# Causal masks of the last four attention units moved from TensorE to GpSimd, with a new instruction order, in an mLSTM plus two-MoE kernel

## The chip, the cores and the metric

One core of a Trainium2 chip runs the whole program. The metric is device time in microseconds (us) of one execution; lower is better. The engines are named as the profile names them: PE is TensorE (matmul), PEld its weight load, DVE is VectorE, ACT is ScalarE, POOL is GpSimd, SP is SyncE, from whose queue nearly all transfers (DMA) are issued.

## What is computed

An mLSTM layer (2 batches, 8 heads, 768 steps, head size 40), then two feed-forward layers on 1536 tokens of width 320. Cut to what matters:

```python
for t in range(S):                                   # attention part, per batch and head
    m_new = np.maximum(f_gate[:, :, t] + m, i_gate[:, :, t])
    f_stab = np.exp(f_gate[:, :, t] + m - m_new)
    i_stab = np.exp(i_gate[:, :, t] - m_new)
    C = f_stab * C + i_stab * outer(v_t, k_t)
    n = f_stab * n + i_stab * k_t
    y[:, :, t] = sigmoid(o_t) * (C @ q_t) / max(abs(n @ q_t), 1)
h = (x @ w1) * (x @ w2) @ w3                         # first MoE, x = y with heads joined
x = h @ w_out
h = x @ w_in                                         # second MoE
out = (h * tanh(softplus(h))) @ w_out2
```

All is float32. The kernel does not step through time: it cuts the 768 steps into 6 chunks of 128 and treats each chunk of a batch as masked attention plus a carried state.

## The kernel before

**Attention units.** There are 12 units, u = 0 to 11 (chunk u // 2 of batch u % 2), built by `add_unit`. The nodes of a unit, each a short list of instructions on one engine:

- `E` (PE): two products of 128x512 (`psE`, L469) that give the logarithms of the decay weights. Ahead of each stands a mask product (L468): the identity times a tile `causal`, which holds -1e30 where a key is later than a query. `dw` (ACT, L474) takes their exponential into the tile `w`.
- `S` (PE, L495): 8 products of keys and queries. `wg` (DVE, L499 to L501, shown as `w<-psS,w`) multiplies them into `w`, 2 instructions.
- `I` (PE, L506, L509): the carried state times the queries; `Ie` (DVE) scales it into `y`. `dx` (ACT) is a small exponential beside it.
- `vw` (POOL, L488) and `U` (PE, L520): the update of the state; `st` (DVE) applies it.
- `Y` (PE, L544): 8 products of `w` and the values; `cb` adds them to `y`.
- `r1`, `r2`, `r3` make 1/denominator; `xs` and `xo` (L572, L576, shown as `x<-y,sg` and `x<-x,r`) multiply `y` by the gate and by it; `dup` (ACT) copies a piece; `X` (PE, L588) transposes; `Xe` (ACT) and `Xl` (DVE) split the result in a high and a low part, which together carry float32 through products of a shorter type.

S, I, U and Y are plain float32: each of their matmuls stands twice in the trace, so a unit's 8 products are 16 rows.

**Weights.** `add_piece` loads a block of weights (SP), takes its bits apart (`mag` on ACT or DVE, then `clamp`, `bits1`, `bits2`, `bits` on DVE, L341 to L359, shown as `f`), and writes a high part (`hi`, ACT) and a low part (`lo`, DVE or POOL). There are 8 pieces each of w1 with w2 (`w12`) and of `w_in` (`wi`), 16 of w3 (`th`), 4 of `w_out` (`wo`) and 8 of `w_out2`.

**MoE stages.** `A` and `B` (PE, L903, `psa` and `psb`) are the products with w1 and w2: 8 matmuls of 128x512 each, for 8 blocks of columns and 3 groups of tokens, 24 of each. `Ae` (ACT) and `Be` (DVE) multiply them. `W` (PE, L876, `psw`) forms w3 @ w_out once, 16 runs of 12 matmuls; `X1` (PE, L943 to L948) applies it. `H` (PE, `psh`) and `O` (PE, L1018, `pso`) are the second MoE, 48 of each. The first A needs the attention output of units 0 to 3 only, so A and B of the first groups can stand between attention units.

**The order.** No engine chooses at run time: each runs its instructions in the order in which they were written down. A list scheduler inside the kernel (`Work.plan`, run while the kernel is built) makes that order from the nodes' due times (`TUNE`, plus `OFF`, an offset for single nodes), the engine of each node (`ENG`), and its own table of durations. Buffers (PSUM banks, `w`, `y`, `x`, weight slots) are given out in this order too. Where it sees TensorE idle before the last `X`, it writes in *warm products* (`keep_warm`, L440, `psz`): matmuls on constants whose result nobody reads. They hold up nothing but TensorE itself. `start` sets up constants, gates and their running sums on DVE and ACT.

The mask is chosen once for all units, by `ENG["mask"]` (L415); with any other value the node `ms` (L477 to L480) would set the masked part of `w` to zero on POOL by an affine select, for every unit.

Of the kernel before, what the change touches and what calls it, by code (L numbers as in the profile page):

```python
# [25 lines left out]
TUNE = dict(
    sgg=(2, 4), s_pe=0.0, s_act=0.143, s_dve=0.011, s_pool=0.0, ahead=3, w0n=8, ff=1.0, ph=3.235, a0=1273.88,
    ap=57.866, a_ld=-1806.87, e_e=2472.31, e_s=-765.62, e_r=7598.61, g_ld=-3051.46, g1=-3249.6, g2=-2767.38,
    o_1=-648.47, o_2=1399.95, c_ld=-2830.66, c_wo=6805.57, cp_wo=-37.478, p0=926.72, pp0=-60.314, c_12=-1429.3,
    w0=-11765.87, wp=-55.889, c_w3=286.38, p1=6793.31, pp1=56.325, p2=9829.98, pp2=563.967, x0=4913.06,  # L30
    x_p=-1108.66, x1=-8484.58, x2=-3892.43, xp=64.158, ldn=dict(w12=2, wi=2), c_o2=-6904.63, cp_o2=92.686,
    c_wi=6950.34, c_o3=10828.2, m0=-902.59, mp0=207.175, mp=248.708, m_o=2909.34,
)
# [10 lines left out]
OFF = dict(
    ll_1=3602.0, S_3=-1169.8, bits1_3=539.7, Y_0=2592.5, A_3=938.5, I_5=1807.9, lo_0=696.0, bits_1=575.3,
    Y_5=-246.0, X_5=621.3, r2_5=-605.0, X_6=-62.8, clamp_5=1680.0, S_7=-839.5, U_9=-210.4, B_0=574.8, lo_3=-503.5,
    xo_2=-1171.6, S_9=-129.5, Y_3=-649.9, mag_19=144.5, B_11=69.7, Y_7=74.1, lo_5=-87.0, clamp_7=73.7, r2_1=86.5,
    Xe_1=488.4, Y_2=-478.1, xo_1=-149.9, I_7=-61.8, st_4=404.5, I_4=-135.1, I_9=-47.3, A_13=-236.0, xs_7=31.9,
    X1h_0=-33.6, bits2_11=668.5, Xl_2=151.6, U_2=-118.7, Y_1=100.4, Wl_2=-297.0, U_8=-9.1, clamp_14=178.7,
    hi_1=-81.7,  # L50
)


# [173 lines left out]
def kernel(  # L227
# [219 lines left out]

# [220 lines left out]
    def start():  # L668
# [23 lines left out]
        if pe_mask:  # L692
            z = z_a.tile([128, N], F32, tag="z0", name="z", bufs=1)
            z3 = z.rearrange("a (h t) -> a h t", h=4)
            nc.gpsimd.memset(z, 0.0)
            nc.gpsimd.affine_select(out=z3, in_=z3, pattern=[[0, 4], [1, T]], base=0, channel_multiplier=-1,
                                    compare_op=ALU.is_ge, fill=-1e30)
# [453 lines left out]
```

## Time and profile before

| | us |
|---|---|
| median of 3 runs | 426.21 (423.79 to 426.89) |
| the profiled execution, its own time | 425.27 |
| its span, first to last instruction | 423.5 |
| PE busy | 414.9 (98%) |
| DVE busy | 290.3 (69%) |
| ACT busy | 211.1 (50%) |
| POOL busy | 48.9 (12%) |

The page's share of a busy engine is an average over stages: the attention part fills the first 128 us or so, mixed with A and B; the W and X1 stage reaches to about 230 us; the rest is the second MoE. A matmul's row lasts longer than the time until the next one starts, since matmuls overlap; what one costs is read from one start to the next. PE's clock has two levels, 2.4 GHz (a granted clock of 1.00 in the profile) and 1.2 GHz (0.50).

### The profile page before, as it was taken

What the parts mean: (1) busy time and instruction counts of PE and PEld (TensorE: products, weight loads), DVE (VectorE), ACT (ScalarE), POOL (GpSimd) and SP (SyncE); (2) the same over time, 40 slices, a digit from 0 to 9 for tenths busy, and PEclk for the clock granted to TensorE, in tenths of its full rate; (3) what the DMA queues carried; (4) which work ended last, traced back from release to release, by engine and by line L of the source; (5) the groups of instructions that cost most, each with busy time, mean ns of one, the idle gap of its engine ahead of it and who ended that gap; (6) DMA issues with size and microseconds to landing.
All of it is one profiled execution on the core that took longest, in us unless ns stands there. A gap on an engine that the chain in (4) does not pass through costs nothing.

```text
span 423.5 us, 6459 instructions
## 1 busy us (share of the span) xinstructions
PE 414.9 (98%) x2489; PEld 362.4 (86%) x2489; DVE 290.3 (69%) x543; ACT 211.1 (50%) x379; POOL 48.9 (12%) x41
## 2 busy tenths in 40 slices
PE   8899999999999999999999999999999999999996
PEld 6589788888888898988888888889999999999996
DVE  8999969999659999999899979865113111123221
ACT  8877666552235233232747788887333333333300
POOL 3312141110000000000001421354000000000000
PEclk9999999999899999999999999999999999999999
DMA  7947464443201543444435422330001000001001
GB/s 241 326 154 239 146 213 134 123 124 132 83 1 42 158 147 111 140 125 149 130 113 180 142 81 77 107 120 23 0 2 62 2 0 2 0 2 62 2 0 63
DMA packets 31647, 41.88 MB, mean 99 GB/s; under 512 B 1856, under 2 KB 25792, under 8 KB 31616
## 3 DMA queue, kind: packets, MB, share of 16 engines
q1 hardware_dynamic: 31040, 41.00, 30.4%
q10 hardware_dynamic: 576, 0.48, 0.3%
q8 instruction: 19, 0.31, 0.3%
q14 instruction: 12, 0.10, 0.1%
HBM read 39.50 MB, written 1.97 MB: 98 GB/s over the span
## 4 chain that ended last, share of the span: by engine, by line
PE 93%; DVE 5%; DMA 1%; issue 0%; ACT 0%; ACTq 0%; DVEq 0%
PE psh L903 21%; PE pso L1018 20%; PE psa L903 11%; PE psb L903 10%; PE psw L876 7%; PE psY L544 5%; PE psx L943 3%; PE psx L945 3%; PE psx L944 3%; PE psS L495 2%; PE psI L506 2%; PE psx L948 1%; PE psx L947 1%; PE psE L468 1%; PE psE L469 1%; PE psX L588 1%
## 5 line engine op out<-in xcount | busy, mean ns | idle before, releaser
L262 DVE TENSOR_TENSOR gl<-u,gh 128x512 fp32r<-128x512 f32 x48 | 33.1, 695 | 84.9 <-PE pso L1018 83.5
L999 ACT ACTIVATE gh<-psh 128x512 fp32r<-128x512 f32 x48 | 28.9, 601 | 64.4 <-PE pso L1018 62.3
L903 PE MATMUL psh<-hs,wih 128*128 128x512 f32 x144 | 56.2, 390 | 0.0
L903 PE MATMUL psh<-hs,wil 128*128 128x512 f32 x144 | 48.2, 389 | 0.0
L1018 PE MATMUL pso<-wo,gh 128*128 128x320 f32 x192 | 42.6, 310 | 0.0
L262 POOL TENSOR_TENSOR wil<-f,wih 128x768 fp32r<-128x768 f32 x8 | 20.1, 2522 | 168.4 <-ACT wih L364 163.2
L903 PE MATMUL psh<-ls,wih 128*128 128x512 f32 x96 | 37.4, 389 | 0.0
L354 DVE SCALAR_TENSOR_TENSOR f<-raw,f 128x768 int32<-128x768 int32 (+2 forms) x44 | 36.9, 840 | 0.4
L359 DVE SCALAR_TENSOR_TENSOR f<-raw,f 128x768 int32<-128x768 int32 (+2 forms) x44 | 36.0, 818 | 0.4
L1003 ACT ACTIVATE u<-psh 128x512 f32<-128x512 f32 x48 | 28.9, 602 | 10.9 <-DVE gl L262 10.7
L1018 PEld LDWEIGHTS pso<-wo,gh 128*128 128x128 f32 x192 | 32.8, 188 | 1.3
L903 PEld LDWEIGHTS psh<-hs,wil 128*128 128x128 f32 x144 | 27.0, 188 | 5.6
L903 PEld LDWEIGHTS psh<-hs,wih 128*128 128x128 f32 x144 | 27.0, 188 | 4.6
L903 PE MATMUL psa<-hs,w12h 128*128 128x512 f32 x72 | 28.8, 400 | 1.1 <-DVE st L262 1.1
L1018 PE MATMUL pso<-wo2h,gh 128*128 128x320 f32 x96 | 29.8, 310 | 0.0
L1018 PE MATMUL pso<-wo2l,gh 128*128 128x320 f32 x96 | 29.7, 309 | 0.0
L1018 PE MATMUL pso<-wo,gl 128*128 128x320 f32 x96 | 29.7, 309 | 0.0
L1018 PE MATMUL pso<-wo2h,gl 128*128 128x320 f32 x96 | 29.7, 309 | 0.0
L345 DVE TENSOR_SCALAR f<-f 128x768 f32<-128x768 f32 (+2 forms) x44 | 23.1, 525 | 9.1 <-ACT f L339 8.8
L903 PE MATMUL psb<-hs,w12h 128*128 128x512 f32 x72 | 28.5, 395 | 0.0
L876 PE MATMUL psw<-woh,th 128*128 128x320 f32 x128 | 28.4, 309 | 0.0
L339 ACT ACTIVATE f<-raw 128x768 f32<-128x768 f32 (+1 forms) x28 | 23.9, 857 | 7.2 <-POOL w12l L262 3.7
(141 smaller groups left out, 939.5 us busy)
## 6 DMA issues: line engine op xcount, KB each, us to landing
raw<-in_w_dram SPq DMA_DIRECT2D x16, 512.0 KB, 3.4
...
```

Source lines behind the costliest of these rows:

```text
L262: return eng.tensor_tensor(out=o, in0=a, in1=b, op=op)
L339: nc.scalar.activation(out=t["f"].bitcast(F32), in_=t["raw"][:, :, 1].bitcast(F32), func=AF.Abs)
L345: nc.vector.tensor_scalar(out=ff, in0=ff, scalar1=HI_MIN, scalar2=HI_MAX, op0=ALU.max, op1=ALU.min)
L354: nc.vector.scalar_tensor_tensor(out=f, in0=t["raw"][:, :, 1], scalar=-0x40000000, in1=f, op0=ALU.bitwise_and, op1=ALU.bitwise_or)
L359: nc.vector.scalar_tensor_tensor(out=f, in0=t["raw"][:, :, 0], scalar=29, in1=f, op0=ALU.logical_shift_right, op1=ALU.bitwise_or)
L544: nc.tensor.matmul(ps[:, h * VW:(h + 1) * VW], lhsT=t["w"][:, h, :], rhs=t["v"][:, h, :], start=True, stop=True)
L876: nc.tensor.matmul(ps, lhsT=t[a][:, 0, c * 128:(c + 1) * 128], rhs=wo[b], start=(c0 + c + s == 0), stop=(c0 + c == KC - 1 and s == 2))
L903: nc.tensor.matmul(ps, lhsT=a, rhs=b, start=(n == 0), stop=(n == len(seq) - 1))
L943: nc.tensor.matmul(x1ps[e], lhsT=wh, rhs=ph, start=first, stop=False)
L999: nc.scalar.activation(out=t["gh"], in_=t["ps"], func=AF.Mish)
L1003: nc.scalar.activation(out=t["u"], in_=t["ps"], func=AF.Mish)
L1018: nc.tensor.matmul(ps, lhsT=t[a][:, sl], rhs=wo[b], start=(ft == 0 and n == 0), stop=(ft == KF2 - 1 and n == 2))
```

## The change

Per unit instead of for all: units 0 to 7 keep the mask product, units 8 to 11 lose it and get the affine select on POOL, between `dw` and `wg`. All tables of numbers are replaced, and with them the order of the whole program. `ENG` puts 24 products `xs`, `xo` from DVE on POOL, the 16 low parts of w3 from DVE on POOL, their `mag` from DVE on ACT, three of four `w12` low parts of POOL on DVE, the four last `w_out2` low parts from POOL on DVE, and some smaller ones. `ahead` (how many units S may run ahead of Y) goes from 3 to 1.

```diff
 TUNE = dict(
-    sgg=(2, 4), s_pe=0.0, s_act=0.143, s_dve=0.011, s_pool=0.0, ahead=3, w0n=8, ff=1.0, ph=3.235, a0=1273.88,
+    sgg=(2, 4), mu=8, s_pe=0.0, s_act=0.297, s_dve=0.0, s_pool=0.006, ahead=1, w0n=5, ff=0.935, ph=3.275,
...
 ENG = dict(
-    mag_w12='ACT', mag_wo='ACT', mag_w3='DVE', mag_wi='ACT', mag_o2='ACT', mag_o3='ACT', lo_w12='DVE', lo_wo='DVE',
-    lo_w3='DVE', lo_wi='POOL', lo_o2='DVE', lo_o3='POOL', xo='DVE', vw='POOL', dup='ACT', mask='PE', rb0='DVE',
-    rc0='DVE', rb1='DVE', rc1='DVE', rb='ACT', rc='ACT', st0='DVE', cb0='ACT', prep='ACT', g_tt='DVE', g_ll='POOL',
+    mag_w12='ACT', mag_wo='ACT', mag_w3='ACT', mag_wi='DVE', mag_o2='DVE', mag_o3='DVE', lo_w12='DVE', lo_wo='DVE',
+    lo_w3='POOL', lo_wi='POOL', lo_o2='DVE', lo_o3='DVE', xo='POOL', vw='POOL', dup='ACT', rb0='DVE', rc0='DVE',
+    rb1='DVE', rc1='DVE', rb='ACT', rc='ACT', st0='DVE', cb0='DVE', prep='ACT', g_tt='DVE', g_ll='DVE',
...
 OFF = dict(
-    ll_1=3602.0, S_3=-1169.8, bits1_3=539.7, Y_0=2592.5, A_3=938.5, I_5=1807.9, lo_0=696.0, bits_1=575.3,
+    bits1_1=1857.6, r1_2=1671.9, B_0=279.9, U_4=2091.4, I_9=257.0, B_2=1762.7, ll_1=1243.5, bits2_1=175.8,
...
-    pe_mask = ENG["mask"] == "PE"
     causal = att.tile([128, 512], F32R, name="causal")
-    if pe_mask:
-        identr = att.tile([128, 128], F32R, name="identr")
-        zr = z_a.tile([128, N], F32R, tag="z1", name="zr", bufs=1)
-    else:
-        identr, zr = causal[:, 0:128], causal
+    identr = att.tile([128, 128], F32R, name="identr")
+    zr = z_a.tile([128, N], F32R, tag="z1", name="zr", bufs=1)
...
     def add_unit(u, due):
         kb, b, c, j = unit_of(u)
         more = c < NCH - 1
+        pe_mask = u < K["mu"]
```

The rest of the diff drops the tests of `pe_mask` in `start`. What it does to the order is shown at three places.

The first is PE at the start of the attention part, from the 8 products `S` of unit 0 to `Y` of unit 0 (`psg` are small transposes of the gates' sums, `psz` warm products). Before:

```order
L495 MATMUL psS<-qk_78 128x128 x8
L440 MATMUL psz<-causal,identr 128x512 x4
L791 MATMUL psg<-ident,gates 128x16
L440 MATMUL psz<-causal,identr 128x512 x4
L791 MATMUL psg<-ident,gates 128x16 x4
L440 MATMUL psz<-causal,identr 128x512 x6
L495 MATMUL psS<-qk_79 128x128 x8
L440 MATMUL psz<-causal,identr 128x512 x2
...
L440 MATMUL psz<-causal,identr 128x512 x2
L520 MATMUL psU<-vw,kv 40x41 x8
L440 MATMUL psz<-causal,identr 128x512 x4
L520 MATMUL psU<-vw,kv 40x41 x8
L544 MATMUL psY<-kv,w 128x41 x8
```

Left out there are the four matmuls of E of unit 2. Now:

```order
L502 MATMUL psS<-qk_78 128x128 x8
L446 MATMUL psz<-causal,identr 128x512 x6
L795 MATMUL psg<-ident,gates 128x16
L446 MATMUL psz<-causal,identr 128x512 x2
L795 MATMUL psg<-ident,gates 128x16 x4
L446 MATMUL psz<-causal,identr 128x512 x5
L527 MATMUL psU<-vw,kv 40x41 x8
L446 MATMUL psz<-causal,identr 128x512 x7
L551 MATMUL psY<-kv,w 128x41 x8
L502 MATMUL psS<-qk_79 128x128 x8
```

Y of unit 0 now stands ahead of S of unit 1, of E of unit 2 and of U of unit 1.

The second is PE late in the attention part, at E of unit 11. Before, behind the A of block 8:

```order
L544 MATMUL psY<-kv,w 128x41 x16
L468 MATMUL psE<-causal,identr 128x512
L469 MATMUL psE<-ex_r_91,ex_l_89 128x512
L468 MATMUL psE<-causal,identr 128x512
L469 MATMUL psE<-ex_r_91,ex_l_89 128x512
L588 MATMUL psX<-ident,x 128x128 x3
L506 MATMUL psI<-st_80,qk_78 128x82 x4
L495 MATMUL psS<-qk_78 128x128 x8
```

Now, between the A of block 3 and the A of block 4:

```order
L551 MATMUL psY<-kv,w 128x41 x8
L502 MATMUL psS<-qk_79 128x128 x8
L476 MATMUL psE<-ex_r_91,ex_l_89 128x512 x2
L513 MATMUL psI<-st_80,qk_78 128x82 x4
```

The two Y that stood together (units 9 and 8) are apart, the mask products are gone, and the attention part ends after 7 A and 2 B instead of after 10 A and 9 B.

The third is POOL, from the `vw` of unit 7 on (numbers are those of buffers). Before, this is all that is left of the attention part there:

```order
L262 TENSOR_TENSOR vw_797<-kv_732,w_676 128x328
L262 TENSOR_TENSOR w12l_765<-f_578,w12h_764 128x768
L262 TENSOR_TENSOR vw_960<-kv_768,w_912 128x328
L262 TENSOR_TENSOR vw_1027<-kv_817,w_1001 128x328
L262 TENSOR_TENSOR w12l_1136<-f_1025,w12h_1135 128x768
```

Now:

```order
L272 TENSOR_TENSOR vw_795<-kv_746,w_675 128x328
L486 AFFINE_SELECT w_768<-w_768 128x8x127
L272 TENSOR_TENSOR x_788<-x_788,r_771 128x320
L272 TENSOR_TENSOR vw_858<-kv_790,w_768 128x328
L272 TENSOR_TENSOR x_773<-x_773,r_680 128x320
L272 TENSOR_TENSOR x_927<-y_865,sg_261 128x320
L486 AFFINE_SELECT w_907<-w_907 128x8x127
L272 TENSOR_TENSOR vw_953<-kv_816,w_907 128x328
L272 TENSOR_TENSOR x_927<-x_927,r_933 128x320
L486 AFFINE_SELECT w_1037<-w_1037 128x8x127
```

The masks and the products `x` now share POOL's queue with `vw`. Over the whole program the number of warm products goes from 40 (8 on zeros, 5 more before the first E, 27 behind it) to 39 (5, 7 and 27), and that of ACT's loads of a function table from 16 to 6.

## Rows read from the trace of the kernel before

**Rows 1.** The page: busy time of each engine, its share, its instructions

```profile
PE 414.9 (98%) x2489; PEld 362.4 (86%) x2489; DVE 290.3 (69%) x543; ACT 211.1 (50%) x379; POOL 48.9 (12%) x41
```

**Rows 2.** Chain that ended last, pieces in order of time: start us, us, what

```profile
35.79 0.36 PE psX L588 x3
...
49.18 0.44 PE psU L520 x16
...
115.59 0.93 PE psI L506 x8
116.52 1.09 PE psS L495 x16
...
119.96 1.71 PE psY L544 x16
...
127.59 5.44 PE psa L903 x24
...
398.45 21.14 PE pso L1018 x144
```

**Rows 3.** Timeline of PE, E of unit 1: start us, us, engine, line, operation, out<-in

```profile
8.30 0.40 PE L469 MATMUL psE<-ex_r,ex_l 128*128 128x512 f32 x1
...
8.54 0.39 PE L468 MATMUL psE<-causal,identr 128*128 128x512 f32 x1
```

**Rows 4.** Timelines of DVE and PE at the first Y: start, us, then the instruction

```profile
21.16 1.28 DVE L262 TENSOR_TENSOR w<-psS,w 128x512 f32<-128x512 f32 x2
...
22.50 1.98 PE L544 MATMUL psY<-kv,w 128*128 128x41 f32 x16
```

**Rows 5.** Stretches: us, PE busy, PEld, DVE, ACT, POOL (count), clock, DMA

```profile
21.16:49.77 28.61, 28.18 (x293) 23.94 (x292) 27.96 (x66) 19.46 (x52) 5.34 (x5) 1.00 0.61 196
...
128.00:200.00 72.00, 72.00 (x377) 63.46 (x376) 68.82 (x139) 25.38 (x44) 0.00 (x0) 1.00 0.41 128
```

**Rows 6.** Groups of DVE by form: count, busy us, mean ns, idle before

```profile
L354 DVE SCALAR_TENSOR_TENSOR f<-raw,f 128x768 int32<-128x768 int32 x16 | 16.1, 1008 | 0.1
L262 DVE TENSOR_TENSOR w<-psS,w 128x512 f32<-128x512 f32 x24 | 15.3, 680 | 0.2
L345 DVE TENSOR_SCALAR f<-f 128x768 f32<-128x768 f32 x16 | 10.0, 626 | 4.8 <-ACT f L339 4.8
L262 DVE TENSOR_TENSOR st<-st,d 128x328 f32<-128x328 f32 x8 | 4.7, 591 | 0.0
```

**Rows 7.** Groups of POOL by form

```profile
L262 POOL TENSOR_TENSOR vw<-kv,w 128x328 f32<-128x328 f32 x10 | 9.3, 937 | 39.2 <-DMA kv<-in_kv_dram 15.1 <-ACT w L474 12.9 <-ACT x L581 5.7
L696 POOL TENSOR_SCALAR_AFFINE_SELECT z<-z 128x512 f32<-128x512 f32 x1 | 0.6, 636 | 0.1
```

**Rows 8.** Timelines of POOL, then of DVE at the same times

```profile
28.23 1.26 POOL L262 TENSOR_TENSOR vw<-kv,w 128x328 f32<-128x328 f32 x1 [5.66 <-ACT x L581]
36.75 0.75 POOL L262 TENSOR_TENSOR vw<-kv,w 128x328 f32<-128x328 f32 x1 [7.26 <-DMA kv<-in_kv_dram]
39.71 1.84 POOL L262 TENSOR_TENSOR w12l<-f,w12h 128x768 fp32r<-128x768 f32 x1 [2.21 <-ACT w12h L364]
...
28.80 1.11 DVE L349 TENSOR_SCALAR f<-f 128x768 int32<-128x768 int32 x1
...
40.59 1.32 DVE L262 TENSOR_TENSOR st<-st,d 128x328 f32<-128x328 f32 x1
```

**Rows 9.** Timeline around the longest wait of PE in the attention part

```profile
59.78 1.28 ACT L484 ACT_TABLE_LOAD   x1
...
64.17 0.47 PE L903 MATMUL psa<-hs,w12h 128*128 128x512 f32 x1 [1.09 <-DVE st L262]
```

**Rows 10.** Timeline of PE and one stretch, where the clock falls

```profile
103.01 3.70 PE L544 MATMUL psY<-kv,w 128*128 128x41 f32 x32
106.51 0.78 PE L468 MATMUL psE<-causal,identr 128*128 128x512 f32 x1
...
106.50:110.00 3.50, 3.50 (x15) 3.01 (x15) 2.02 (x6) 2.18 (x6) 0.00 (x0) 0.51 0.65 206
```

More of the change, by code (lines that the diff above doesn't have):

```diff
@@ L26 @@
 TUNE = dict(
-    sgg=(2, 4), s_pe=0.0, s_act=0.143, s_dve=0.011, s_pool=0.0, ahead=3, w0n=8, ff=1.0, ph=3.235, a0=1273.88,
[L28 to L32, printed above, removed]
+    sgg=(2, 4), mu=8, s_pe=0.0, s_act=0.297, s_dve=0.0, s_pool=0.006, ahead=1, w0n=5, ff=0.935, ph=3.275,
+    a0=-12.81, ap=-93.853, a_ld=-1652.39, e_e=8363.2, e_s=3345.95, e_r=2252.59, g_ld=6316.58, g1=-2898.98,
+    g2=-4276.68, o_1=-7529.36, o_2=8885.52, c_ld=3037.46, c_wo=1113.52, cp_wo=108.045, p0=-952.74, pp0=59.804,
+    c_12=-11722.61, w0=1316.87, wp=-59.276, c_w3=-13157.38, p1=-662.73, pp1=33.908, p2=704.76, pp2=572.165,
+    x0=-2337.92, x_p=2487.93, x1=-2214.51, x2=2869.52, xp=-139.242, ldn=dict(w12=2, wi=2), c_o2=88.35,
+    cp_o2=12.531, c_wi=-5894.32, c_o3=-2264.6, m0=-1939.09, mp0=-162.897, mp=204.465, m_o=1263.83,
 )
 ENG = dict(
-    mag_w12='ACT', mag_wo='ACT', mag_w3='DVE', mag_wi='ACT', mag_o2='ACT', mag_o3='ACT', lo_w12='DVE', lo_wo='DVE',
-    lo_w3='DVE', lo_wi='POOL', lo_o2='DVE', lo_o3='POOL', xo='DVE', vw='POOL', dup='ACT', mask='PE', rb0='DVE',
-    rc0='DVE', rb1='DVE', rc1='DVE', rb='ACT', rc='ACT', st0='DVE', cb0='ACT', prep='ACT', g_tt='DVE', g_ll='POOL',
-    lo_w120='DVE', lo_w121='POOL', lo_w122='POOL', lo_w123='POOL', lo_w124='DVE', lo_w125='DVE', lo_w126='POOL',
+    mag_w12='ACT', mag_wo='ACT', mag_w3='ACT', mag_wi='DVE', mag_o2='DVE', mag_o3='DVE', lo_w12='DVE', lo_wo='DVE',
+    lo_w3='POOL', lo_wi='POOL', lo_o2='DVE', lo_o3='DVE', xo='POOL', vw='POOL', dup='ACT', rb0='DVE', rc0='DVE',
+    rb1='DVE', rc1='DVE', rb='ACT', rc='ACT', st0='DVE', cb0='DVE', prep='ACT', g_tt='DVE', g_ll='DVE',
+    lo_w120='DVE', lo_w121='DVE', lo_w122='DVE', lo_w123='DVE', lo_w124='DVE', lo_w125='POOL', lo_w126='DVE',
     lo_w127='DVE',
@@ L44 @@
 OFF = dict(
-    ll_1=3602.0, S_3=-1169.8, bits1_3=539.7, Y_0=2592.5, A_3=938.5, I_5=1807.9, lo_0=696.0, bits_1=575.3,
[L46 to L50, printed above, removed]
+    bits1_1=1857.6, r1_2=1671.9, B_0=279.9, U_4=2091.4, I_9=257.0, B_2=1762.7, ll_1=1243.5, bits2_1=175.8,
+    Xl_3=-34.5, Ie_3=350.2, st_3=653.8, wg_0=-368.4, r2_3=-499.9, xs_7=342.0, bits_1=537.6, lo_17=267.2, Ie_6=14.4,
+    Y_1=153.4, bits_36=-9.5, ll_2=22.8, pl_1=-8.7, gl_16=-54.9, B_1=-31.4, clamp_4=-335.2, Mh_20=-18.8,
+    Mu_22=-20.2, clamp_14=304.0, lo_3=-68.3, lb0_1=-3.8, clamp_3=4.7, S_7=-95.4, lo_0=-1.7, lo_26=7.0, Be_3=4.5,
+    clamp_13=-3.8, Xl_8=-117.4, Xe_8=-0.8, mag_7=23.9, less_2=-9.2, rb_5=3.9, xs_2=-32.2, Ae_4=181.5, pb_1=-50.0,
+    Ie_5=-181.8, la0_0=122.4, load_5=-153.3, Xl_2=22.6, lb0_0=-2.3, turn_1=-61.1, bits1_4=-74.2, Mu_21=49.6,
+    load_15=-14.0, bits1_2=-3.3, Ph_9=-73.0, r3_3=-101.3, wg_4=-25.5, dx_3=5.4, ld_kv_5=-4.8, B_14=-2.3,
+    lo_21=-27.3, cb_0=9.1, gl_40=1.7, X_11=-125.6, dup_0=596.4, rc_5=-3.4, gl_35=-20.0, U_0=2.9, dw_0=-52.0,
+    gl_13=93.9, Ae_3=18.6, bits2_0=-41.1, Be_8=-77.1, A_1=-125.0, rb_0=-27.9, O_14=-1.3, bits_22=-163.2,
+    bits1_0=103.8, bits2_9=195.8, H_3=-57.2, r2_5=-53.5, H_25=98.4, ld_kv_11=-81.2, turn_2=44.2, E_3=12.0,
+    Ae_1=-139.9, clamp_0=25.0, wg_1=0.8, dw_1=157.3, I_10=14.4, Ie_4=36.4, A_19=10.2, mag_21=-371.3, Mu_25=-28.1,
+    B_3=-11.8, hi_0=139.7, pa_1=5.3, dx_4=12.0, S_3=-5.2, X_5=-138.4, X_2=10.5, r1_3=25.6, rb_1=-101.6,
+    lb0_2=217.2, mag_26=-0.1, H_36=-2.1, cb_1=-1.7, rb_2=-78.8, S_11=34.7, hi_26=1.7, H_39=-71.3, la1_1=-20.8,
+    cb_9=-19.7, Pl_17=-4.5, vw_1=4.6, ld_o_5=35.9, Mh_2=3.4, mag_3=-6.7, clamp_21=2.6, te_2=23.8, E_5=-3.4,
+    X_8=-7.6, dup_2=-22.4, bits_43=10.4, ld_kv_2=-100.6, B_5=-4.4, Mu_32=-13.7, mag_0=-203.3, xs_8=-172.1,
+    Xl_0=-3.2, cb_5=-2.0, B_4=-274.7, dw_2=4.1, pr_1=216.9, clamp_43=271.6, Ae_0=-4.0, la0_2=49.1, bits_20=-43.2,
 )
@@ L691, in start @@
         keep_warm(K["w0n"], zr[:, 0:128], zr)
[L692 to L697, printed above, removed]
+        z = z_a.tile([128, N], F32, tag="z0", name="z", bufs=1)
+        z3 = z.rearrange("a (h t) -> a h t", h=4)
+        nc.gpsimd.memset(z, 0.0)
+        nc.gpsimd.affine_select(out=z3, in_=z3, pattern=[[0, 4], [1, T]], base=0, channel_multiplier=-1,
+                                compare_op=ALU.is_ge, fill=-1e30)
         nc.gpsimd.memset(qk[1][:, 0], 0.0)
-        if pe_mask:
-            nc.scalar.copy(identr, ident)
+        nc.scalar.copy(identr, ident)
         low, top = slice(0, 64), slice(64, 128)
@@ L717, in start @@
         prep_r(0)
-        if pe_mask:
-            nc.scalar.copy(causal, z)
+        nc.scalar.copy(causal, z)
         for b in range(B):
```

## The prediction

> **What bounds the kernel now.** I read the page first, then the chain that ended last, then the timelines of the first 128 us. TensorE is busy in 98% of the span [rows 1], and the chain runs along it almost without a break. From 127.59 us on it is closed: an A takes 5.44 / 3 = 1.81 us, piece after piece, down to the last O, which ends at 398.45 + 21.14 = 419.6 us [rows 2]. DVE is busy in 68.8 of the 72 us from 128 to 200 and still holds nobody up there [rows 5]. So the end is TensorE's work plus its waits, and all waits lie ahead of 128 us: first the gates, until the first Y at 22.50 us [rows 4], then the attention units. In those DVE is the partner: from 21.16 to 49.77 us it is busy for 27.96 of 28.61 us [rows 5], and its `w<-psS,w` products gate each Y.
>
> How much does TensorE wait among the units? Take the stretch from the first Y (22.50) to the twelfth (119.96) [rows 2, 4], 97.5 us. By the order it holds 11 Y, 10 S, 9 E, 10 I, 8 U, 11 X and 19 A or B. Prices, all from one piece's start to the next: Y 1.71, S 1.09, U 0.44, X 0.36, I 0.93 (1.0 with its small product), A or B 1.81 [rows 2]; a product of E 0.24, from the starts 8.30 and 8.54 [rows 3], so an E with masks 0.96. That is 18.8 + 10.9 + 8.6 + 10.0 + 3.5 + 4.0 + 34.4 = 90.2 us of work, and 7.3 us of waits. Two of these have a name: 1.1 us at 64.17 us, where an A waits for a state update of DVE, behind a table load of 1.28 us on ACT [rows 9]; and the fall of the clock at 106.5 us, behind two Y in a row (32 matmuls, 3.7 us) [rows 10]. For 3.5 us the granted clock is 0.51, the lower of its two levels; at most half of that is lost, about 1.5 us.
>
> **The change, part by part.** *Mask products.* Eight products of E go, on the path: 8 x 0.24 = 1.9 us less. The warm products (40, now 39) stand in waits and count for nothing by themselves.
>
> *The start.* Ahead of the first `w` product DVE has five instructions fewer (six go behind it, and the low part of a gate comes from POOL), each a few tenths: some 2 us earlier. But TensorE has done less by its first Y: S of unit 1, E of unit 2 and one U now stand behind it, 1.09 + 0.96 + 0.44 = 2.5 us. Between 0 and 0.5 us are lost; I take 0.3.
>
> *The units.* By the order the same stretch, first to twelfth Y, now holds 11 Y, 11 S, 6 E with masks and 4 without, 10 I, 9 U, 8 X and only 9 A or B: 18.8 + 12.0 + 7.7 + 10.0 + 4.0 + 2.9 + 16.3 = 71.7 us. The ten A or B that went out do not vanish, they run densely behind the units; but they were also what DVE had to catch up in. What has DVE to do between the first and the twelfth pair of `w` products? 145 instructions: 22 `w` at 0.68, 14 `f` of the dearer kind at 1.01 and 16 of the cheaper at 0.63 [rows 6], 6 low parts near 1.0 (they are as wide as the dear `f`), 2 `a` as wide as `w`: 15.0 + 14.1 + 10.1 + 6 + 1.4 = 46.6 us, and 85 smaller ones. The smaller ones I price from the dense stretch of before: 28.61 us for 66 instructions, of which 10 `w`, 4 dear and 5 cheap `f` and a low part make 14.9 us, so 13.7 us for 46, or 0.30 each, waits between instructions included. 85 x 0.30 = 25.5, together 72 us. DVE and TensorE thus need the same time, 72 us, where before TensorE had 90 us of work against a DVE with some 184 instructions. That the `x` products left DVE is counted in this.
>
> *POOL.* They went to POOL, whose operations collide with DVE's. A `vw` takes 0.75 us alone, but 1.26 beside a DVE instruction that itself took 1.11, where the cheap `f` have a mean of 0.63; a `st<-st,d` of DVE, 0.59 in the group's mean, took 1.32 beside a low part on POOL [rows 6 to 8]. Both DVE instructions take all their inputs from SBUF. In the dense stretch POOL was busy 5.3 of 28.6 us, 19% [rows 5], and it cost DVE these two delays, (1.11 - 0.63) + (1.32 - 0.59) = 1.2 us, or 23% of POOL's time. Now POOL has in the 72 us: 20 `x` at 0.73 (`vw` scaled from 328 to 320 columns), 9 `vw` at 0.75, a low part at 1.84, and 4 masks. No affine select of this size is in the trace; one of 512 columns takes 0.64 us, and the mask has 8 x 127 = 1016, so it costs between 0.64 and 1.27, and I take 1.1, near the width it has. That makes 14.6 + 6.8 + 1.8 + 4.4 = 27.6 us, 38%. The 14 us above the old 19% cost DVE another 14 x 0.23 = 3.2 us. Both ends: nothing, if each lies beside PSUM work of DVE or an idle DVE, and 14 us x 0.55 = 7.7 us more than now if each operation of POOL that meets an SBUF instruction of DVE (some 55% of DVE's 72 us: `f` and low parts 30 us, and 32 of the small ones, 10 us) holds it up in full. The masks themselves wait behind `x` and `vw` in POOL's queue, and behind each mask wait the same unit's `vw`, then U, and its `w` products; three A or B stand on TensorE between E and Y of units 8 and 9, one to two for units 10 and 11, so a mask that is 1 to 2 us late is covered there.
>
> So the waits in the new stretch: DVE is 72 + 3.2 - 71.7 = 3.5 us over TensorE, the seven warm products written into it mark 7 x 0.24 = 1.7 us of waits on chains of single steps, and a fall of the clock may stay, 1.5: together 6.7, against 7.3 now. 0.6 us are won.
>
> *Table loads.* Ten loads of 1.28 us [rows 9] leave ACT, which is no bound; the one that ended in TensorE's 1.1 us is in the 7.3 already. Now a load stands ahead of `dw` of unit 8, with an A and a B, 3.6 us, behind that E as cover.
>
> *Later stages.* In the W stage DVE gives up 16 `mag` and 16 low parts of w3, POOL takes the low parts, at 0.75 x 512 / 328 = 1.2 us each or 19 us in all. If every one held DVE up, that would about equal the 16 x (0.4 + 0.7) = 18 us that DVE is rid of, so that its 3 us of slack per 72 stay; the price is taken as 0. Transfers: the first 24 rows of SP's queue are the same, and later ones are issued by the same releases.
>
> **The sum.** -1.9 (masks) + 0.3 (start) - 0.6 (waits) = -2.2 us. The profiled execution took 425.27 us for a span of 423.5, so 423.1 now. It lies 0.9 us under the median of 426.21; on the median the change gives 424.0 us.
>
> **Rivals.** *Faster: DVE keeps up.* POOL's operations find cover, the clock does not fall since no two Y stand together any more, and only the 1.7 us of marked waits remain: 7.3 - 1.7 = 5.6 us won instead of 0.6, 419.0 us. For it: DVE's instruction list is not longer than TensorE's, and DVE waits for PSUM results in between, when POOL is free to run. Against it: two engines with equal loads do not overlap without loss; before, DVE was full for 28 us and TensorE waited then too.
>
> *Slower: POOL blocks DVE in full.* From the upper bound above: 7.7 us instead of 3.2, and since DVE then falls behind at each unit, the last `w` products, on which the twelfth Y and all A and B behind it wait, come that much later: 4.5 us more, 428.5; with a second fall of the clock 430. It becomes slower than before once the waits of the stretch exceed 7.3 - 0.3 + 1.9 = 8.9 us, and by over 1% once they exceed 13.2. Rows 8 speak for it: the `st<-st,d` that started at 40.59 ended only after POOL's operation had, at 41.55. The Trainium skill states this as a rule (SBUF — State Buffer, section "Who interferes with whom"): a DVE instruction with two SBUF inputs and a GpSimd one that reads SBUF exclude each other, and the second fully blocks; by it the time would be this rival's, and the trace agrees in both collisions named, while the `vw` of 0.75 us at 36.75 shows that one without a meeting is not delayed. Against the full price: half of DVE's work reads PSUM.
>
> *Slower: a low part on POOL late in the W stage.* A low part of w3 takes 1.2 us instead of 0.7 and stands between ACT's high part and W; if the buffered pieces don't cover 0.5 us for each of 16, TensorE loses up to 8 us: 432.
>
> **How the numbers follow.** A measurement of this kernel can tell about 1%, 4.3 us, from no change. My forecast, within that, has 0.55, and its own range is 421.9 to 427. DVE keeping up has 0.29, and all but 0.01 of that lies below 421.9. The blocked DVE has 0.11 and the W stage 0.05; they end between 427 and 432, and 0.10 of their 0.16 lie above 430.5, where a fall of the clock comes on top. So faster 0.28, same 0.62, slower 0.10. The range reaches from 418.5, the faster rival, to 429.5, the blocked DVE without more clock falls.
>
> **What would show it.** Eight `psE` matmuls fewer, and the first Y 2 to 2.5 us earlier than 22.5: right on the first two terms. Waits of TensorE for DVE `w` in the stretch of the twelve Y, and DVE at 95% or more in it: the forecast's 6.7 us; no such waits and DVE under 85%: the faster rival. DVE's `f` and `st<-st,d` groups well above 0.63 and 0.59 us: the blocked DVE. Waits of `psw` for the low parts of w3 between 130 and 210 us: the W stage. It is wrong in its base if TensorE is not closed behind the last unit.

## The result and the profile after

The changed kernel takes 420.85 us (median of 8 runs, 419.17 to 426.7) where the kernel before, run beside it, takes 425.59 (8 runs). The ratio is 0.9894, with a 95% interval of 0.9871 to 0.9917: 1.06% faster, 4.5 us, at the edge of the 1% that I had taken as what can be told from no change. The profiled execution went from 425.27 to 421.06 us, its span from 423.5 to 419.1. The forecast was 2.2 us, or 424.0 from a base of 426.21; it gave itself 421.9 to 427, and 420.85 lies below that, in the part of the whole range that stood for the faster rival.

One fact is needed to read the numbers below: in some executions the granted clock falls for a few us among the units, in others it doesn't. Without a fall the span is 417.2 to 417.6 us for after (3 of its 14 executions) and 421.8 to 422.6 for before; with one it is 418.5 to 419.9 and 423.3 to 424.4; a few executions at a mean clock of 0.992 or less are longer still. Spans are compared below at like clocks.

The page of after, with the granted clock in 40 slices:

```profile
PE 411.6 (98%) x2480; PEld 361.6 (86%) x2480; DVE 290.6 (69%) x513; ACT 193.0 (46%) x367; POOL 81.9 (20%) x77
PEclk9999999899999999999999999999999999999999
```

TensorE (PE) is busy for 3.3 us less, GpSimd (POOL) went from 48.9 to 81.9 us, DVE stayed at 290 [rows 1]. Stretches of after (columns as in [rows 5]):

```profile
18.34:97.07 78.73, 77.99 (x720) 68.87 (x720) 72.25 (x148) 52.43 (x119) 34.30 (x33) 0.98 0.55 171
74.63:78.04 3.41, 3.41 (x15) 3.21 (x15) 3.16 (x5) 2.15 (x6) 1.54 (x1) 0.50 0.80 238
128.00:200.00 72.00, 72.00 (x385) 64.13 (x385) 58.99 (x99) 30.97 (x54) 20.84 (x16) 1.00 0.40 130
```

The first is the stretch from the first to the twelfth Y, 78.7 us where the prediction had 71.7 of work and 6.7 of waits. The second is the fall of the clock to the lower of its two levels; in before it lay at 106.5 us [rows 10]. In the third TensorE is never idle, as before, but DVE has 59.0 busy us instead of 68.8. The chain of after, two pieces behind the units:

```profile
109.41 9.07 PE psa L907 x40
...
403.25 12.34 PE pso L1022 x84
```

It is closed behind the units: 5 A in 9.07 us, and the last O ends at 415.6 us, where before has 419.6 [rows 2]. The start on DVE, then on TensorE (timelines of after):

```profile
14.68 0.90 DVE L272 TENSOR_TENSOR gates<-gates 32x512 fp32r<-32x512 f32 x2
15.61 0.74 DVE L787 SCALAR_TENSOR_TENSOR ex_l<-gates,neg_b,ex_l 32x512 fp32r<-32x512 f32 x1
16.38 1.12 DVE L272 TENSOR_TENSOR ex_r<-gates,sel_h 64x512 fp32r<-64x512 f32 x1
...
17.54 1.29 DVE L272 TENSOR_TENSOR w<-psS,w 128x512 f32<-128x512 f32 x2
...
18.34 0.36 PE L551 MATMUL psY<-kv,w 128*128 128x41 f32 x2
```

The first w product comes at 17.54 us and the first Y at 18.34, 3.6 and 4.2 us earlier than in [rows 4]; the prediction had 2 and 2 to 2.5. The groups of POOL in after (by form: count, busy us, mean ns, idle before):

```profile
L272 POOL TENSOR_TENSOR x<-x,r 128x320 f32<-128x320 f32 x12 | 12.0, 1001 | 9.7 <-DVE r L574 9.5
L272 POOL TENSOR_TENSOR x<-y,sg 128x320 f32<-128x320 f32 x12 | 11.0, 922 | 21.9 <-DVE y L272 7.7 <-issue 5.7 <-PE psX L595 5.6
L486 POOL TENSOR_SCALAR_AFFINE_SELECT w<-w 128x1016 f32<-128x1016 f32 x4 | 5.4, 1341 | 12.3 <-ACT w L481 12.3
```

A mask costs 1.34 us (I took 1.1), an x product 0.92 to 1.00 (I took 0.73). So meetings can lengthen POOL's instructions too, as the `vw` of 1.26 us beside 0.75 alone in [rows 8].

### The profile page after: what moved, and what is told of

It is laid out like the page before. It is cut to its first block, busy times and chain, and to the rows that moved or that the text cites. A ratio compares the mean times of both kernels' runs of the same rounds, so it can differ in the third digit from the quotient of the medians.

```text
span 419.1 us, 6450 instructions
## 1 busy us (share of the span) xinstructions
PE 411.6 (98%) x2480; PEld 361.6 (86%) x2480; DVE 290.6 (69%) x513; ACT 193.0 (46%) x367; POOL 81.9 (20%) x77
## 4 chain that ended last, share of the span: by engine, by line
PE 93%; DVE 5%; issue 1%; DMA 1%; ACT 0%; ACTq 0%; DVEq 0%
PE psh L907 21%; PE pso L1022 20%; PE psa L907 11%; PE psb L907 10%; PE psw L880 7%; PE psY L551 5%; PE psx L947 3%; PE psx L948 3%; PE psx L949 3%; PE psS L502 3%; PE psI L513 2%; PE psx L952 1%; PE psx L951 1%; PE psE L476 1%; PE psX L595 1%; DVE gates L272 1%
## 5 line engine op out<-in xcount | busy, mean ns | idle before, releaser
L272 DVE TENSOR_TENSOR gl<-u,gh 128x512 fp32r<-128x512 f32 x48 | 36.3, 758 | 86.9 <-ACT u L1007 84.2
L364 DVE SCALAR_TENSOR_TENSOR f<-raw,f 128x768 int32<-128x768 int32 (+2 forms) x44 | 39.5, 900 | 0.8 <-DVE r L571 0.3
L369 DVE SCALAR_TENSOR_TENSOR f<-raw,f 128x768 int32<-128x768 int32 (+2 forms) x44 | 38.1, 870 | 0.4
L272 POOL TENSOR_TENSOR th<-f,th 128x512 fp32r<-128x512 f32 x16 | 21.9, 1370 | 67.7 <-ACT th L374 54.3
L272 POOL TENSOR_TENSOR wil<-f,wih 128x768 fp32r<-128x768 f32 x8 | 16.3, 2033 | 67.2 <-ACT wih L374 67.1
L349 ACT ACTIVATE f<-raw 128x512 f32<-128x512 f32 (+2 forms) x28 | 21.3, 760 | 16.4 <-POOL th L272 12.5
```

The source lines that it names most:

```text
L272: return eng.tensor_tensor(out=o, in0=a, in1=b, op=op)
L349: nc.scalar.activation(out=t["f"].bitcast(F32), in_=t["raw"][:, :, 1].bitcast(F32), func=AF.Abs)
L364: nc.vector.scalar_tensor_tensor(out=f, in0=t["raw"][:, :, 1], scalar=-0x40000000, in1=f, op0=ALU.bitwise_and, op1=ALU.bitwise_or)
L369: nc.vector.scalar_tensor_tensor(out=f, in0=t["raw"][:, :, 0], scalar=29, in1=f, op0=ALU.logical_shift_right, op1=ALU.bitwise_or)
```

## Experiments

All keep the order of the instructions of the kernel that they start from, except the two named w_first, and warm_two, which adds two warm products; the planner's tables are left alone, and in the others only the engine of one step is changed where it is issued.

**The low part of the gates, both ways.** From after, with this line on GpSimd as shown; from before, with `nc.vector` in its place.

```diff
-            gtt(c0, "ll", L2[96:128, sl], ...)
+            tt(nc.gpsimd if c0 >= 2 else nc.vector, L2[96:128, sl], ...)
```

> The kernel after, with one instruction moved back: the low part (32x512) of the gates of the last four chunks goes to GpSimd again, at its place in the order; every other engine's list stays. In the kernel before it took 1.71 us there and stood beside a DVE instruction of 1.27 us that alone takes 0.29. Theory 'the start is on the path': the first w product and the first Y come 1 to 2 us later than 17.54 and 18.34 us, and so does the end: span 420.1 to 421.1 us against 419.1. Rival 'the start is absorbed by the waits of the units': the first Y comes later by the same amount, but the twelfth Y stays at its 97.07 us within 0.3, and the span at 419.1 within 0.3.

Measured: span 418.0 us, ratio to before 0.9904 [0.9874, 0.9933]. POOL, then DVE in this run (timelines):

```profile
14.24 1.29 POOL L272 TENSOR_TENSOR gates<-gates 32x512 fp32r<-32x512 f32 x1 [9.55 <-DMA raw<-in_w_dram]
...
14.25 1.43 DVE L272 TENSOR_TENSOR gates<-gates 32x128 fp32r<-32x128 f32 x1
...
18.08 1.29 DVE L272 TENSOR_TENSOR w<-psS,w 128x512 f32<-128x512 f32 x2
```

The 32x128 instruction of DVE takes 1.43 us and ends 0.15 us behind POOL's. Yet the first w product is only 0.54 us later, since DVE is rid of 0.6 us of its own. All Y up to the eighth (71.9 against 71.4 us) keep that delay. This execution had no fall of the clock, and two more at a mean clock of 0.999 to 1.000 have 418.4 and 418.7; against 417.2 to 417.6 of after without a fall the three are 0.4 to 1.5 us longer. The ratios can't tell the run from after. So the start is on the path in the profile, as the first theory says, but this part moved the first Y by a third of what I expected.

> The kernel before, with one instruction moved: the low part (32x512) of the gates of the last four chunks goes from GpSimd to DVE, at its place in the order. Theory 'meetings on SBUF': in before it takes 1.71 us on GpSimd and meets DVE's gates 32x128 (1.27 us instead of 0.29), and the vw behind it meet ex_r and ex_l (1.19 and 1.12 instead of 0.69 and 0.74); on DVE it costs 0.6 us itself and the meetings mostly go, so the first w product comes 0.5 to 1.2 us before 21.16 us, and the span ends as much earlier, 422.3 to 423.0 us against 423.5. Rival 'the order, not the meetings': the low part on DVE costs what it saves, the first w product stays at 21.16 within 0.3; then the 3.6 us by which it is earlier in after come from the five instructions alone that went behind it.

Measured: first w product at 20.89 us instead of 21.16, TensorE's end 0.44 us earlier, lowest spans 421.6 to 421.8 against 421.9; ratio 0.9986 [0.9969, 1.0003]. At the start that is nearly the rival: the low part costs DVE nearly what the meeting cost.

**The masks, both ways.** From after, E with mask products for all units and no select:

```diff
-                if pe_mask:
+                if True:
                     nc.tensor.matmul(t["E"][e], lhsT=identr, rhs=causal, start=True, stop=False)
...
         def ms():
+            return
```

> The kernel after, with the four masks taken off GpSimd and the eight mask products of units 8 to 11 back on TensorE, at the places of their E; the order is otherwise that of after. Theory 'masks are on the path': 8 x 0.24 = 1.9 us more, span 421.0 us. Rival 'masks lie in waits': the units' stretch has 7.0 us of waits, the products fill them, and the span stays at 419.1. Second rival, by the clock: in after the granted clock falls from 74.63 to 78.04 us, right behind Y, S and the two products of an E; four products there instead of two keep it up, which gives back 1.5 us: span 419.5, and no fall of the clock near 75 us in the trace.

Measured: median 420.20 us, ratio 0.9893 [0.9866, 0.9921]; that is the ratio of after, 0.9894. Four of six executions had no fall of the clock, with spans of 417.7 to 418.3, up to 1.1 us above after's. TensorE at the E of unit 8 and one stretch (timeline, windows):

```profile
62.83 0.50 PE L475 MATMUL psE<-causal,identr 128*128 128x512 f32 x1
...
63.87 0.40 PE L908 MATMUL psa<-hs,w12h 128*128 128x512 f32 x1
...
72.00:82.00 10.00, 10.00 (x86) 9.05 (x86) 9.23 (x22) 5.18 (x11) 1.69 (x2) 1.00 0.63 196
```

In after this A starts at 63.99, held by DVE's y; here, behind two products more, at 63.87. The wait took them. And the clock stays at 1.00 from 72 to 82 us. That isn't shown to be the products' doing: it also stays at 1.00 there in the profile of the run above, with the low part on GpSimd, and in a second one of after (the run after_same, below), which have no product more in that stretch. So the eight products are there to be saved, and saving them brings nothing that the medians show, and at most 1.1 us without a fall: a part was waiting time anyway. Whether they help to hold the clock stays open. The span came out at none of the three theories' numbers.

From before, the masks alone:

```diff
             (at the end of dw)
+            if u >= 8:
+                w = t["w"][:, :, 0:T - 1]
+                nc.gpsimd.affine_select(out=w, in_=w, pattern=[[0, H], [1, T - 1]], ...)
```

> The kernel before, with the masks of units 8 to 11 set on the exponentials by GpSimd, right behind the exponential in GpSimd's list, and their eight mask products gone from TensorE; the order is otherwise that of before. Theory 'masks on the path' (the forecast's term): 8 x 0.24 = 1.9 us less, span 421.6 us. Rival 'half of it falls into waits': in after, putting the products back cost 1.1 us only, since a wait of 0.7 us at one E took two of them; then 0.8 to 1.2 us less here, span 422.3 to 422.7. Second rival, by the clock: with fewer columns between the Y and the S the granted clock falls once more, and 0.5 us or less is left.

Measured: median 426.49 us, ratio 1.0049 [1.0030, 1.0068]: 2.1 us slower; the profiled span is 424.5 us. All three expectations had a gain. POOL, DVE and TensorE (timelines), and the stretch where the clock falls in before:

```profile
69.86 1.13 POOL L478 TENSOR_SCALAR_AFFINE_SELECT w<-w 128x1016 f32<-128x1016 f32 x1 [8.82 <-ACT w L474]
95.25 1.10 POOL L478 TENSOR_SCALAR_AFFINE_SELECT w<-w 128x1016 f32<-128x1016 f32 x1 [2.27 <-ACT w L474]
...
69.97 1.83 DVE L359 SCALAR_TENSOR_TENSOR f<-raw,f 128x768 int32<-128x768 int32 x1
95.52 0.86 DVE L568 TENSOR_SCALAR r<-r 128x8 f32<-128x8 f32 x1
...
73.40 0.50 PE L907 MATMUL psa<-hs,w12h 128*128 128x512 f32 x1 [0.49 <-DVE w L262]
86.50 0.73 PE L907 MATMUL psa<-hs,w12l 128*128 128x512 f32 x2 [0.79 <-DVE w12l L262]
97.85 0.52 PE L592 MATMUL psX<-ident,x 128*128 128x128 f32 x3 [1.80 <-DVE x L262]
...
106.50:110.00 3.50, 3.50 (x31) 3.35 (x31) 2.79 (x7) 0.67 (x3) 0.00 (x0) 1.00 0.93 332
```

Beside the first select an f takes 1.83 us, one that takes 0.94 at 94 us in the same run; beside the other an instruction of DVE on 8 columns stands still for 0.86 us until the select is over at 96.35. DVE's list is late behind both, with its w, w12l and x, and TensorE waits 0.5 + 0.8 + 1.8 = 3.1 us, three waits that before doesn't have, where it was rid of 1.9. That is 1.2 us more. The span is 1.0 us longer than the profile of before, but that one has a fall of the clock from 106.5 us on [rows 10], some 1.5 us, and this execution has none there. At like clocks (424.4 to 424.5 at a mean of 0.998 to 0.999, against 421.8 to 422.6) the run is about 2 us longer, so the named waits account for some half of it; 0.4 us stand ahead of the first Y already (22.87 against 22.50), and the rest isn't traced.

**x on GpSimd, both ways.** `nc.gpsimd if ENG["xo"] == "POOL" else nc.vector` becomes `nc.vector` (from after) or `nc.gpsimd` (from before), in both x products.

> The kernel after, with the 24 x products of the units on DVE instead of GpSimd, each at its place in the order. Theory of the forecast: DVE and TensorE have equal work in the stretch from the first to the twelfth Y (18.34 to 97.07 us); 20 x products at some 0.4 us add 8 us to DVE and return the collisions of 20 x 0.73 x 0.23 = 3.4 us, so the stretch gets 4 to 5 us longer and the span 423 to 424 us. Rival 'GpSimd blocks DVE in full': what returns is 20 x 0.73 x 0.55 = 8 us, the time stays at 419.1 within 0.5, and the st<-st,d and f groups of DVE, 0.668 and 0.752 us in after, fall back to about 0.59 and 0.63. Second rival 'DVE has slack here': its groups stay and the span too, and DVE's idle time in the stretch shrinks by 8 us.

Measured: span 424.4 us, lowest 423.0; median 428.93, ratio 1.0071 [1.0036, 1.0105]. One stretch and the two groups of DVE between 18 and 100 us (windows, then groups by form):

```profile
18.10:100.30 82.20, 80.18 (x720) 70.08 (x720) 77.52 (x165) 52.62 (x119) 14.50 (x13) 0.96 0.53 165
...
L272 DVE TENSOR_TENSOR x<-y,sg 128x320 f32<-128x320 f32 x9 | 4.8, 528 | 0.0
L272 DVE TENSOR_TENSOR x<-x,r 128x320 f32<-128x320 f32 x9 | 4.7, 527 | 0.0
```

From the first to the twelfth Y it is 82.2 us instead of 78.7, and the profiled span lies 0.4 us above the theory's 423 to 424. Part of the longer stretch is the clock: its mean is 0.96 instead of 0.98, by my estimate 1.7 us, and TensorE is idle for 2.0 us instead of 0.7. At like clocks (0.995 to 0.996) the lowest span of 423.0 stands against 418.5 to 419.9 of after: 3 to 4.5 us. Eight of the twelve had a mean clock of 0.980 to 0.988 and spans of 426.5 to 430.1, so the median is 8 us above after's, which no theory had. DVE's busy time grew from 72.25 to 77.52 us, 5.3, for 17 instructions more of 0.53, 9.0 us: 3.7 came back, which I put down to meetings, for 34.30 - 14.50 = 19.8 us less of POOL, 0.19 per us. The prediction had 0.23; blocking in full would have been 0.55. The group `st<-st,d` went from 0.668 to 0.626 us and `f` from 0.752 to 0.741, not down to the rival's 0.59 and 0.63.

> The kernel before, with the 24 x products of the units on GpSimd instead of DVE, each at its place in the order; masks, order and all other engines as in before. It is the counterpart of x_on_dve, which put them back in after and cost some 5 us. Theory 'x on GpSimd is the gain': from 21 to 50 us DVE is full in before (27.96 of 28.61 us) and holds eight of these products, 0.48 us each; with them gone the units of that stretch run 1.5 to 3 us shorter, and the span is 420.5 to 422 us where before has 423.5 with one fall of the clock and 422.0 without. Rival 'only in this order': in the order of before DVE's list is not what holds TensorE beyond 50 us, each x on GpSimd takes 0.9 to 1.0 us instead of 0.48 and comes later to X and to its A and B, so the gain of the first stretch is given back: span 423.5 within 0.7.

Measured: median 425.65 us, ratio 1.0026 [1.0008, 1.0045]. None of its 12 executions is free of a fall of the clock, where 10 of the 17 of before beside it are; at like clocks the spans are the same (423.5 to 424.4 against 423.3 to 424.4). The sixth Y came 1.0 us earlier (52.35 against 53.30), but the A of [rows 9] 0.15 us later. POOL, ACT and TensorE (timelines), then a stretch:

```profile
50.54 1.04 POOL L262 TENSOR_TENSOR x<-y,sg 128x320 f32<-128x320 f32 x1 [4.58 <-ACT sg L659]
...
52.55 1.45 POOL L262 TENSOR_TENSOR vw<-kv,w 128x328 f32<-128x328 f32 x1
56.75 1.84 POOL L262 TENSOR_TENSOR w12l<-f,w12h 128x768 fp32r<-128x768 f32 x1 [2.75 <-ACT w12h L364]
...
58.63 0.92 ACT L339 ACTIVATE f<-raw 128x768 f32<-128x768 f32 x1 [1.81 <-POOL w12l L262]
...
64.32 0.76 PE L903 MATMUL psa<-hs,w12h 128*128 128x512 f32 x1 [1.17 <-DVE st L262]
...
64.00:68.00 4.00, 3.68 (x9) 2.98 (x10) 3.24 (x6) 1.62 (x6) 1.45 (x1) 0.57 0.55 166
```

An x product stands at the head of POOL's list waiting for the sigmoid of ACT until 50.54, and a vw waits behind it. The low part of w12 is held by something else: POOL stands idle for 2.75 us until ACT's high part is there. Behind the low part waits ACT's next f. The A waits for the same state update as in before, and then the clock falls, from 64 to 68 us. So the 1.0 us are given back by 64 us; by which of these waits is not shown. The theory holds for the first stretch and the rival for the whole. In x_on_dve the new order without x on GpSimd is slower than before. So neither the order of after nor x on GpSimd brings the gain without the other.

**The low parts of w3.** In `low()`, `lo_e == "POOL"` becomes `lo_e == "POOL" and kind != "w3"`.

> The kernel after, with the 16 low parts of w3 on DVE instead of GpSimd, at their places in the order. The forecast set this part's price at nothing, since TensorE waits for nobody behind the units: DVE goes from 59 busy us of the 72 from 128 to 200 us to some 65, and the span stays at 419.1 within 0.4. Rival 'the low parts on GpSimd bring some of the gain': then TensorE gets waits for them on DVE between 100 and 200 us and the span is 1 to 4 us longer.

Measured: span 418.8 us, median 420.21, ratio 0.9893 [0.9853, 0.9933], no difference from after; TensorE is busy for 72.00 of the 72 us from 128 to 200. The price of nothing was right.

**The fall of the clock.** Two warm products ahead of the S of unit 8:

```diff
         def S_():
+            if u == 8:
+                keep_warm(2)
```

> The kernel after, with two warm products (128x512, 0.23 us each) ahead of the S of unit 8, between the Y that starts at 71.4 us and the E that starts at 74.4. In after the granted clock falls to 0.51 or so from 74.63 to 78.04 us and TensorE loses about 1.4 us by it. Theory 'the clock falls for want of columns there': no fall near 75 us, which gives 1.4 us for 0.46: span 418.1 against 419.1, and a clock of 1.00 in most runs. Rival 'the fall has another cause or another place': the fall stays or moves by one piece, span 419.5 or more.

Measured: spans 417.6 to 417.9 in three executions, 419.1 to 419.4 in three; ratio 0.9898 [0.9877, 0.9919]. Two stretches of the profiled one (windows):

```profile
18.00:30.00 12.00, 12.00 (x120) 10.48 (x118) 10.93 (x22) 9.43 (x21) 3.65 (x5) 0.93 0.75 223
...
72.00:82.00 10.00, 10.00 (x86) 9.05 (x87) 9.71 (x20) 5.24 (x11) 2.54 (x2) 1.00 0.71 224
```

The clock stays at 1.00 from 72 to 82 us, as the first theory says, but it is down at the first Y instead, and the span is 419.1. That the two products did either is not shown. The kernel after, unchanged, did the same in the profile of after_same (below), span 418.6 us (windows):

```profile
16.00:18.00 2.00, 2.00 (x21) 1.17 (x19) 1.94 (x4) 1.99 (x3) 1.03 (x1) 0.50 0.91 323
...
72.00:82.00 10.00, 10.00 (x92) 9.22 (x91) 9.81 (x20) 4.95 (x10) 2.80 (x3) 1.00 0.73 223
```

So the fall has another place in another execution of one and the same kernel, and a single profile can't tell whether an edit moved it.

> The kernel after, with the masks of units 8 and 9 back on TensorE (four products) and those of units 10 and 11 on GpSimd. If the wait of 0.7 us behind the E of unit 8 (63.05 us) takes the first two products, and the two at the E of unit 9 (74.4 us) keep the clock up, this costs 0.5 us and gives 1.4: span 418.0 to 418.3, and the clock at 1.00 in most runs. Rival 'each product costs its 0.24 us': span 419.5 to 420.1.

Measured: median 419.31 us, 7 of 12 spans at 417.1 to 417.5; ratio 0.9891 [0.9860, 0.9921]. Where the clock held, the four products cost nothing against 417.2 to 417.6 of after; the expected gain at the second place isn't shown. In the profiled execution (418.8 us) it fell between 82 and 100 us, where the mean is 0.91. The median is the lowest of all runs, but its interval covers after's, so a better kernel isn't shown.

**The first Y still earlier.** On DVE the w products of unit 0 go ahead of the gates' scans; on TensorE Y of unit 0 goes ahead of the transposes of the gates and S of unit 1 behind them.

```diff
+        for what, ahead in [(("vw", 0), ("pb", 1)), (("wg", 0), ("pc", 1)), (("Y", 0), ("te", 1)), (("S", 1), ("less", 2))]:
+            r = next(r for r in rows if r[2] == what)
+            rows.remove(r)
+            rows.insert(next(i for i, x in enumerate(rows) if x[2] == ahead), r)
```

> The kernel after, unchanged, on the same chip as the two below, to compare them with it: span 418.5 to 419.5 us where the clock falls once, 417.2 where it does not.

> The kernel after with the start in another order: DVE's two w products of unit 0 go ahead of the scans of the gates (from 17.5 to about 12.5 us), and on TensorE Y of unit 0 and S of unit 1 go into the stretch from 13 to 18 us in which warm products (128x512) stand. Nothing that E of unit 2 waits for (ex_l and ex_r on DVE, till 21.4 us in after) is moved back by it. Theory 'the start is TensorE's': the 2.8 us of Y and S come out of the path up to the point where E of unit 2 becomes ready, which is 0.3 to 1.2 us before the 21.66 us of after: the second Y and the end come 0.5 to 1.2 us earlier, span 417.9 to 418.6 us with one fall of the clock. Rival 'DVE is the bound there': its list is as long as before, so the second w product stays at 22.4 us, the second Y at 24.2 us and the span at 419.1 within 0.3, although the first Y comes 4 us earlier.

> The start of the run w_first together with the masks of units 8 and 9 on TensorE (the run masks_8_9, whose spans lay at 417.1 to 417.5 us where the clock did not fall). If both add up: 416.0 to 416.8 us without a fall of the clock. If DVE bounds the start: 417.3 within 0.3.

Measured: after, as the run after_same, 417.3 to 419.1 us, ratio 0.9876 [0.9838, 0.9914]; w_first 425.45 us in the median, lowest span 419.7, ratio 0.9959 [0.9916, 1.0001]; w_first_8_9 423.80, lowest 419.8, 0.9968 [0.9937, 0.9999]. Both theories fail. TensorE and the clock in w_first (timeline, windows):

```profile
12.93 0.42 PE L556 MATMUL psY<-kv,w 128*128 128x41 f32 x2 [0.44 <-DVE w L277]
...
19.53 2.50 PE L451 MATMUL psz<-causal,identr 128*128 128x512 f32 x5
...
24.28 0.39 PE L480 MATMUL psE<-causal,identr 128*128 128x512 f32 x1
...
15.00:18.00 3.00, 2.67 (x14) 1.76 (x15) 2.28 (x5) 1.14 (x4) 1.11 (x1) 0.59 0.98 331
18.00:21.00 3.00, 3.00 (x20) 2.48 (x19) 1.43 (x2) 2.97 (x4) 0.00 (x0) 0.50 1.04 276
```

The first Y comes at 12.9 us, 5.4 earlier, and the E of unit 2 at 24.28 instead of 21.66. Two things stand between. The clock is at its lower level from about 15 to 22 us, so that five warm products take 2.50 us; in after_same, where the warm products were left in place, it is down too, but only from about 15 to 18.5. And the scans, with them ACT's part of the gates, come later, and DVE waits 2.6 us for U, which stands behind those warm products. What each of the two costs was not run apart. So the first Y by itself is no measure of the start.

## Why the prediction was right, and where its size was off

The direction was right and the size half of what was measured. The median lies in the whole range only because that reached down to the faster rival, whose mechanism did not happen: that much is luck. Of the 3.2 us between 424.0 and 420.85, 0.6 are the base, which has 425.59 in eight executions and 426.21 in the prediction's three. By terms, in the two profiles: start - 1.7, masks - 1.9, the units' waits - 0.1 to - 0.3, tail - 0.4, some 4.2 of 4.4 us. That counts where time went in the traces; what a part brings by itself is a matter of the runs, and there the masks brought next to nothing.

*The base held.* TensorE's work plus waits, closed behind the units: the last O ends 4.0 us earlier, which is the start, the masks and the units; the rest of the span's 4.4 us is the tail behind it, 3.9 to 3.5 us.

*The start is the term that was mis-sized:* + 0.3 us forecast, - 4.2 + 2.5 = - 1.7 measured. The 2.5 us of TensorE's work that moved behind the first Y were right; what failed is the price of DVE's instructions, "each a few tenths: some 2 us". The rows of before (timeline of DVE) show it:

```profile
14.96 1.27 DVE L262 TENSOR_TENSOR gates<-gates 32x128 fp32r<-32x128 f32 x1
16.26 1.19 DVE L262 TENSOR_TENSOR ex_r<-gates,sel_h 64x512 fp32r<-64x512 f32 x1
17.48 1.12 DVE L783 SCALAR_TENSOR_TENSOR ex_l<-gates,neg_b,ex_l 32x512 fp32r<-32x512 f32 x1
18.61 0.69 DVE L262 TENSOR_TENSOR ex_r<-gates,sel_h 64x512 fp32r<-64x512 f32 x1
19.34 0.74 DVE L783 SCALAR_TENSOR_TENSOR ex_l<-gates,neg_b,ex_l 32x512 fp32r<-32x512 f32 x1
20.09 0.56 DVE L345 TENSOR_SCALAR f<-f 128x768 f32<-128x768 f32 x1
20.68 0.56 DVE L349 TENSOR_SCALAR f<-f 128x768 int32<-128x768 int32 x1
```

From one start to the next, ex_r, one ex_l and the two f take 0.73 + 0.75 + 1.07 us, two small ex_l ahead of these rows 0.63; 0.61 for the low part of the gates come in: 2.6 us. The other 1.0 us go with POOL, in meetings that the prediction didn't look for at the start: the 32x128 takes 1.27 us (0.28 in after), ex_r 1.19 (0.69), ex_l 1.12 (0.74), together 1.9 us over; in after two meetings are left, with 0.9. The sum, 3.6, is what the first w product gained. This split is worked out from the rows; run by itself is only the low part, 0.3 to 0.5 us. The 4.2 us at the first Y hold for this execution. In after_same, where the clock falls ahead of it, the first Y starts at 19.93 us, 2.6 earlier than in before, and the first w product at 17.22: what DVE gained is there in both.

*The masks:* the count was right (40 psE matmuls in the order instead of 48) and so was 0.24 us each, but not that they are a gain of their own. With them back the median is the same; moved alone into the old order they cost 2.1 us. "On the path" was true of the products, and the prediction left out that what follows can wait for DVE as soon as they are gone, as the A at 63.99 us does for 0.54.

*The units' waits held in number:* 6.7 us forecast, 78.7 - 71.7 = 7.0 measured. (The 7.3 of before takes the start of the twelfth Y from the chain; the timeline's 119.80 makes it 7.1.) What filled them is in part not what was forecast. The sign for it was waits of TensorE for DVE's `w` and DVE at 95% or more. All waits of TensorE in the stretch (waits of after):

```profile
PE psa L907 <- DVE y L272: 0.5, 1, 0.5
PE psY L551 <- DVE w L272: 0.2, 1, 0.2
```

TensorE waits 0.2 us for a `w`, and DVE is busy for 72.25 of 78.73 us, 92%, between the two signs. The warm products are there, seven in the order, and so is the fall of the clock with its 1.5 us; the 3.5 us of DVE are not seen as waits, and some 3 us between the pieces stay unnamed. So that this sum came out is partly luck. The reason given for the fall, two Y in a row, was too narrow: in after it comes behind one Y and one S,

```profile
71.42 1.96 PE L551 MATMUL psY<-kv,w 128*128 128x41 f32 x16
73.31 1.16 PE L502 MATMUL psS<-qk 40*128 40x128 f32 x16
74.40 0.62 PE L476 MATMUL psE<-ex_r,ex_l 128*128 128x512 f32 x1
```

and in other executions elsewhere (in after_same ahead of the first Y) or not at all.

*POOL's price held*, 0.19 against 0.23 per us, and so did the value of moving x, which shows only in the new order. Of the two collisions that the prediction holds against the rule on two SBUF inputs, only the `st<-st,d` has two; the `f<-f` has one. The Trainium skill (SBUF — State Buffer, "Who interferes with whom") says that the second of two fully blocks, and it also counts one-input instructions of DVE in a two-port mode among those that meet GpSimd, which the prediction did not use. Single rows agree (0.86 us for an r on 8 columns beside a select). The rival built on it failed as a price for all of POOL's time: DVE lost 0.19 us per us, and the x products of POOL themselves took 0.92 to 1.00 us. Its sign came only in part: `st<-st,d` takes 0.668 us in after.

*The faster rival*, DVE keeping up, gave 419.0 us, and the time lies between it and the forecast. Its mechanism is not what happened: the fall stayed, and the stretch has 7.0 us beyond TensorE's work where the rival had 1.7. *The W stage* cost nothing, as forecast.

What stays open: the new order with none of its four changes of engine (low part, masks, x, w3) wasn't run, only with each of them taken back by itself; nor is it settled what decides in which execution the clock falls, and where.
